# Other memory slots for the gate, staging and product buffers of a planned kernel, and finer cells for its DRAM order

## The chip, the core and the metric

The kernel runs on one core of a Trainium2 chip. The metric is the device time of one execution in microseconds, as the median of several runs. The core has a matrix engine (PE; its weight loads are listed as PEld), a vector engine (DVE), a scalar engine (ACT), a general engine (POOL) and SyncE (SP), whose queue issues nearly all DMA transfers here. Every engine takes its instructions strictly in order, so an instruction that waits holds back everything behind it on that engine.

## The reference

What is computed is attention, then a gated feed-forward layer, then a second feed-forward layer:

```python
# attention, (B, H, S, D) = (4, 8, 576, 64)
scores = where(causal, -1e9, q @ k.T / sqrt(D) + minimum(-(cum[:, None] - cum[None, :]), 0))   # cum = cumsum(max(s, 0))
x = (softmax(scores) @ v) reshaped to (2304, 512)
# layer 1: 512 -> 1536 -> 512
xn = x / sqrt(mean(x * x) + 1e-6) * rms_g
y = (silu(xn @ w_gate) * (xn @ w_val)) @ w_out
# layer 2: 512 -> 2048 -> 512
h = y @ w_in
out = (h / (1 + exp(-1.702 * h))) @ w_out2
```

The weights come as 64-bit floats and are turned into 32-bit floats on the core. Products are made from a high and a low part of each factor, three matmuls for one product.

## The kernel before

The work has two phases. In the first, the 32 heads of attention run, and beside them the first four of the twelve chunks of layer 1 (`G0 = 4`) for tokens 0 to 1727, in seven tiles (`fa_tile`, line 695; tile 6 is the last, 192 tokens wide). Each tile takes tanh on ACT, and writes its result from the buffer `YO` to the DRAM buffer `y_d`, two halves for each tile.

The second phase starts with a job called P: chunk 4 of layer 1 for tokens 0 to 767, straight (8 products, each of 6 matmuls of 384 columns). `gate` takes Silu of a product into one of the two gate buffers `SG0` and `SG1`; `gated` multiplies it with the other product and splits the result into high and low part. Then two matmuls only keep PE going (`ones`), and eight outputs (`Down("P", ...)`, 3 matmuls each) are added to `MK0` and `MK1`, which hold what `y_d` has for these tokens (loaded by two transfers). After P comes R (`run_r`): chunks 0 to 3 for the 576 tokens that the first phase left, in two halves of 288 tokens (`RN`), R0 and R1. At the end of each half four results of 288 tokens, q = 0 to 3, are copied by ACT from PSUM to a staging buffer and written to DRAM (`r_d`). The staging buffers of R0 are `RE`, `M51`, `V1`, `M50` in turn, those of R1 are `RE`, `M51`, `RE`, `M51` (line 1070). Between R1's outputs the first group of the steady part is begun, and that part runs to the end: groups of seven products (`m1` to `m7`, a Strassen form), in which `V1` and the two `M5` buffers carry copies of products. `m3` adds onto the PSUM bank that `m5` has filled, so it can't start before ACT's copy of that bank into `M5` has been made; the next group's `m1` follows `m3`.

Buffers share memory in slots (`SLOTS`, line 32). A slot has turns: its second list of names takes the memory when the first list is no longer used by anyone, which includes DMA transfers that read it. Before, `SG0 SG1` follow `TH0 TH1 YO` in slot `se`; `V1 RE` follow `BT0 BT1` in slot `sa` (`BT` takes half of a head's result from PSUM). Here the names of the profile are those of the slots: `se`, `sa`, `sh` (M5), `sc` (MK), `sb` (the first results of `gated`), `s` for those with a number.

The order of all instructions is made by the program itself, before it emits them. `op` collects what an operation reads and writes as cells (`cells`, 512 bytes in DRAM before, 64 in the on-chip memory), and makes it wait for earlier writers and readers of the same cells and for the users of the turn before in its slot. `plan` then orders the operations on each engine by modelled costs and by the latest time at which each may start. Table loads of ACT have no cost in it; a DMA transfer is modelled as 2.2 us and its bytes at 360 GB/s, one after the other. What the instructions really wait for is worked out separately from the emitted order and the bytes that they touch. The matmuls of the second phase (`tmul`) keep the order in which they are written.

A row of `r_d` is 288 floats, 1152 bytes, and a row of `y_d` 1728 floats, 6912 bytes; neither is a multiple of 512, both are of 128. With cells of 512 bytes the end of a row and the start of the next share a cell.

Of the kernel before, what the change touches and what calls it, by code (L numbers as in the profile page):

```python
# [29 lines left out]
    "VIRT": 260096,  # L30
    "SLOTS": {
# [5 lines left out]
    },  # L37
    "BANK": {"s": (0, 1, 5), "t": (2, 3), "v": (4,), "g": (6,), "o": (7,), "r": (4, 4)}, "BANKX": {"s": (7,), "v": (6,)}, "NX": 8,
    "FB": (0, 1, 2, 3, 4, 5), "BB": (6, 7),
# [8 lines left out]
def attention_then_swiglu_then_gelu(ctx: ExitStack, tc, qT, kT, vp, s, w1, w2, gT, out):  # L48
# [4 lines left out]
    KT = DM // P  # L53
# [9 lines left out]
    H2 = 384  # L63
    NP = NT // (2 * H2)
    RN = (NT - TA) // 2
    NAMES = ["B11", "T1", "T2", "B22", "T3", "B21", "T4"]
# [32 lines left out]
    def few(n):  # L99
# [8 lines left out]
    SHAPE = {  # L108
        "Q": [S], "K": [S], "mask": [S], "SQ": [S], "VS": [5, 2 * D], "PA": [1600], "PT": [512], "VT": [5, 2, D],
        "BT": [320], "XH": [2, TS], "TH": [TS], "FH": [2, TS], "YO": [2, TS], "w": [2, 512], "wb": [512], "ws": [512],  # L110
        "MK": [2, 2, H2], "HH": [2, H2], "M5": [H2], "SG": [H2], "V1": [H2], "RE": [H2], **{nm: [2, 2, H2] for nm in NAMES},
    }
    ROUND = ("QA", "QB", "KA", "KB", "VT", "XH", "FH", "w", "HH", *NAMES)

# [47 lines left out]
    def get(name, n=None):  # L162
        if n is None:
            return BUF[name][0]
        return [BUF[f"{name}{i}"][0] for i in range(n)]

    QS, KS, QB, KB, QA, KA, VS, VT, BT, TH = (get(x, 2) for x in ("QS", "KS", "QB", "KB", "QA", "KA", "VS", "VT", "BT", "TH"))
    mask, SQ, SQT, YO = (get(x) for x in ("mask", "SQ", "SQT", "YO"))
# [3 lines left out]
    WS = [own(f"w{i}", [2, 512], F32R) for i in range(PRM["NWO"])] + [BUF[f"w{i}"][0] for i in range(PRM["NWO"], NWS)]  # L172
    PC = {nm: BUF[nm][0] for nm in NAMES}
    MK, HH, M5, SG = get("MK", 2), get("HH", 8), get("M5", 2), get("SG", 2)
    wb, ws, V1, RE = (get(x) for x in ("wb", "ws", "V1", "RE"))
    FB = [PB[i] for i in PRM["FB"]]
    BB = [PB[i] for i in PRM["BB"]]

# [37 lines left out]
    def size(ap):  # L216
        return 8 if ap.dtype == I64 else 4

    def cells(ap):
        if not hasattr(ap, "offset"):  # L220
            ap = ap[tuple(slice(None) for _ in ap.shape)]
        t, pat, es = ap.tensor.name, tuple(ap.ap), size(ap)
        key = (t, ap.offset, pat, es)
        if key in known:
            return known[key]
        space = str(ap.space)
        if "DRAM" in space and t != virtual.tensor.name:
            offs = [ap.offset * es]
            dims = pat[1:] if pat[0][1] == P else pat
            for st, n in dims[:-1]:  # L230
                offs = [o + st * es * i for o in offs for i in range(n)]
            st, n = dims[-1]
            got = {(t, c) for o in offs for c in range(o // 512, (o + st * es * (n - 1)) // 512 + 1)}
        else:
            pitch, rows = pat[0]
            p0, col = divmod(ap.offset, pitch)
            if "PSUM" in space:
                got = {(t, 0)}
            else:
                offs = [col * es]  # L240
                for st, n in pat[1:-1]:
                    offs = [o + st * es * i for o in offs for i in range(n)]
                st, n = pat[-1]
                half = ([0] if p0 < 64 else []) + ([1] if p0 + rows > 64 else [])
                got = set()
                g = 4 if t == small.tensor.name else 64
                for o in offs:
                    for c in range(o // g, (o + max(st * es * (n - 1), 0) + es - 1) // g + 1):
                        for h in half:
                            got.add((t, c, h))  # L250
                if any(t == x.tensor.name for x in ST):
                    par = [offs[0] // 4 % 2] if st == 2 and es == 4 else [0, 1]
                    got = {x + (y,) for x in got for y in par}
        known[key] = got
        return got
# [51 lines left out]
    def op(eng, fn, cost=None, r=None, w=None, due=None, chain=False, dma=False):  # L307
# [10 lines left out]
        if w is None:  # L318
            for name, kw in rec.calls:
                for k, x in kw.items():  # L320
                    if isap(x):
                        (wr if k in OUTS else rd).update(cells(x))
                if dma:
                    n = size(kw["out"])
                    for x in kw["out"].shape:
                        n *= x
                    o["byts"] += n
        else:
            for x in w:
                wr.update(cells(x))  # L330
            for x in r or ():
                rd.update(cells(x))
# [38 lines left out]
    def cp(o_, i_, scale=1.0, **kw):  # L371
        op("A", lambda e: e.activation(out=o_, in_=i_, func=AF.Copy, scale=scale), **kw)
# [10 lines left out]
    def dma(o_, i_, eng="S", **kw):  # L383
        op(eng, lambda e: e.dma_start(out=o_, in_=i_), dma=True, **kw)
# [533 lines left out]
    def done(b):  # L918
        bank_free.append(b)
# [32 lines left out]
    def add(o_, x, y, o=ALU.add):  # L952
        tt(o_, x, y, o, eng="V")
# [79 lines left out]
    class Down:  # L1033
# [30 lines left out]
        def finish(self, first, final):  # L1064
            self.part(self.chunks)
            b, p, o = self.b, self.p, self.o
            ps = FB[b]
            if self.layer == "R":
                q = o[1]
                t = (RE, M5[1], V1, M5[0])[q % (4 if p == 0 else 2)]  # L1070
                cp(t[:, :RN], ps[:, :RN])
                dma(r_d[p][:, q, :], t[:, :RN])
            elif self.layer == "P":
                t, q = o
                mt = MK[t].rearrange("p a k n -> p (a k) n").bitcast(F32)
                add(mt[:, q, :], ps[:, :H2], mt[:, q, :])
                if q == KT - 1:
                    dma(y_d[:, :, (2 * p + t) * H2:(2 * p + t + 1) * H2], mt)
            elif self.layer == "1":
                t, q = o  # L1080
                y = xT[:, q, (2 * p + t) * H2:(2 * p + t + 1) * H2]
                add(y, ps[:, :H2], y)
            else:
                b0 = p * 2 * H2
                if o < 4:
                    v, src = xT[:, o, b0:b0 + 512], ps[:, :]
                else:
                    k = o - 4
                    v = xT[:, 2 * k:2 * k + 2, b0 + 512:b0 + 768]
                    src = ps.rearrange("p (s f) -> p s f", s=2)  # L1090
                if first:
                    cp(v, src)
                else:
                    add(v, src, v)
                if final:
                    q = p * 6 + o
                    dst = out[q * P:q * P + P, :]
                    dma(dst if o < 4 else dst.rearrange("p (s f) -> p s f", s=2), v)
            done(b)
# [12 lines left out]
    n = 0  # L1112
# [20 lines left out]
    for nm in ("B11", "B21", "B12", "B22"):  # L1133
        k, t = BL[nm]
# [80 lines left out]
    for j, job in enumerate(SJ):  # L1215
        layer, p, cs = job
# [52 lines left out]
    def lat(x, y):  # L1269
        return 0.22 if x != y else 0.0 if x == "T" else 0.06  # L1270

    def length(o):
        return 2.2 + o["byts"] / 360e3 if o["byts"] else min(o["cost"])
# [10 lines left out]
    def plan(asap):  # L1284
# [11 lines left out]
        byasap = {e: sorted((o["i"] for o in ops if e in o["eng"]), key=lambda i: asap[i]) for e in engs}  # L1296
        ptr = {e: 0 for e in engs}
        start, finish, chosen = [None] * N, [None] * N, [None] * N
        count = 0
        stall = []  # L1300
# [10 lines left out]
        while count < N:  # L1311
# [55 lines left out]
            for s_ in o["succ"]:  # L1367
                left[s_] -= 1
                rdy[s_] = max(rdy[s_], finish[i] + lat(e, ops[s_]["eng"]))
                if not left[s_]:  # L1370
                    for k in ops[s_]["eng"]:
                        ready[k].append(s_)
        return start, finish, chosen, stall

    asap = [0.0] * N
    for o in ops:
        t = max([asap[d] + length(ops[d]) + lat(ops[d]["eng"], o["eng"]) for d in o["deps"]], default=0.0)
        asap[o["i"]] = max(t, ideal.get(o["i"], 0.0))
    start, finish, chosen, stall = plan(asap)
    for _ in range(PRM["PASS"]):  # L1380
        start, finish, chosen, stall = plan(start)
# [65 lines left out]
```

## Time and profile before

| | |
|---|---|
| median of 3 runs | 1074.27 us (1073.88 to 1076.59) |
| the profiled execution | 1073.97 us, its span 1072.2 us |
| granted PE clock over the span | 0.987 |
| busy PE, PEld | 1033.4 us (96%), 967.8 us (90%) |
| busy DVE, ACT, POOL | 717.6 us (67%), 577.9 us (54%), 436.9 us (41%) |
| PE not busy | 38.8 us |
| DMA | 165.59 MB, mean 154 GB/s |

The span runs from the first to the last instruction; 1.8 us of the execution lie outside it. The first phase ends at about 350 us, P and R run from there to about 425 us, the rest is the steady part. Nearly all instructions are emitted through one helper, line 206, so a row is told by the tiles that it writes and reads.

### The profile page before, as it was taken

To read this page: it belongs to the slowest core of one execution; us is meant where nothing else is said; L and a number is where in the kernel's file an instruction comes from. 1 tells how busy PE (TensorE), PEld (TensorE's weight loads), DVE (VectorE), ACT (ScalarE), POOL (GpSimd) and SP (SyncE) were. 2 spreads that over 40 slices of the span, in tenths; PEclk is the share of its full clock that TensorE was granted. 3 is DMA by queue.
4 is the path that set the end of the run, shared out by engine and by line. 5 is a ranking of instruction groups with operands and counts; after the bars stand their busy time and mean duration, and the time that the engine had idled before them with its cause. 6 is when DMAs were issued, how large, how long until landed. Compare 5 with 4: busy or idle time off the path is not lost.

```text
span 1072.2 us, 17418 instructions
## 1 busy us (share of the span) xinstructions
PE 1033.4 (96%) x6200; PEld 967.8 (90%) x6200; DVE 717.6 (67%) x1589; ACT 577.9 (54%) x1335; POOL 436.9 (41%) x503
## 2 busy tenths in 40 slices
PE   6998889999999899799999999999999999999998
PEld 4887879999999889799999999999998889999987
DVE  5766878888877756678764678888565377364333
ACT  4776777777776435455433344577563255343222
POOL 5567588878765332535410244543131033030000
PEclk9998999999999989899999999999999999999999
DMA  4334443334311544568275158675255427613551
GB/s 143 101 92 124 143 128 102 88 114 116 98 32 40 171 157 149 202 212 316 62 265 206 40 174 330 246 291 207 98 168 202 160 67 278 225 40 121 206 204 59
DMA packets 59227, 165.59 MB, mean 154 GB/s; under 512 B 6482, under 2 KB 25426, under 8 KB 59140
## 3 DMA queue, kind: packets, MB, share of 16 engines
q1 hardware_dynamic: 59028, 164.40, 44.6%
q8 instruction: 49, 0.80, 0.3%
q14 instruction: 38, 0.31, 0.1%
q10 hardware_dynamic: 112, 0.08, 0.0%
HBM read 117.24 MB, written 44.26 MB: 151 GB/s over the span
## 4 chain that ended last, share of the span: by engine, by line
PE 89%; DVE 4%; DMA 3%; POOL 2%; issue 1%; ACT 1%; SPq 0%; POOLq 0%; ACTq 0%; DVEq 0%
PE b L206 89%; DMA st<-in_w_dram 2%; DVE s L206 1%; POOL s L206 1%; DVE xT L206 1%; DMA s<-s 1%; DMA y_d<-se 0%; DVE se L206 0%; DVE wm L206 0%; DVE sg L206 0%; DVE w L206 0%; DMA s<-c_d 0%; POOL sg L206 0%; ACT w L206 0%; POOL w L206 0%
## 5 line engine op out<-in xcount | busy, mean ns | idle before, releaser
L206 PE MATMUL b<-s,w 128*128 128x384 f32 (+1 forms) x882 | 170.1, 335 | 5.4 <-ACT sh L206 5.4
L206 PEld LDWEIGHTS b<-s,w 128*128 128x128 f32 x882 | 155.0, 190 | 6.4 <-ACT sh L206 5.8
L206 POOL TENSOR_TENSOR wa<-wa,st 128x512 int32<-128x512 int32 x52 | 71.9, 1383 | 205.3 <-ACT sb L206 61.0
L206 DVE TENSOR_TENSOR xT<-b,xT 128x384 f32<-128x384 f32 (+1 forms) x134 | 80.2, 608 | 83.2 <-PE b L206 81.9
L206 PE MATMUL b<-sc,w 128*128 128x256 f32 (+3 forms) x840 | 131.3, 297 | 3.1 <-ACT w L206 2.0
L206 PEld LDWEIGHTS b<-sc,w 128*128 128x128 f32 x840 | 116.1, 193 | 5.1 <-ACT w L206 2.2
L206 PE MATMUL b<-sd,w 128*128 128x256 f32 (+3 forms) x642 | 111.3, 305 | 0.4 <-DVE sd L206 0.3
L206 ACT ACTIVATE b<-b 128x384 f32<-128x384 f32 x119 | 55.6, 479 | 98.5 <-DVE b L206 58.5
L206 POOL TENSOR_SCALAR wm<-wm 128x512 f32<-128x512 f32 x68 | 46.9, 689 | 131.7 <-DVE wm L206 130.4
L206 PE MATMUL b<-s 128*128 128x288 f32 (+4 forms) x384 | 88.2, 357 | 12.7 <-DMA s<-s 9.2
L206 POOL TENSOR_SCALAR s<-s,small 128x576 f32<-128x576 f32 (+4 forms) x160 | 86.3, 558 | 27.3 <-DVE small L206 25.2
L206 PEld LDWEIGHTS b<-sd,w 128*128 128x128 f32 x642 | 96.0, 189 | 1.4 <-DVE sd L206 1.0
L206 ACT ACTIVATE s<-s,small 128x320 f32<-128x320 f32 (+4 forms) x160 | 88.3, 553 | 12.2 <-DVE small L206 11.7
L206 PE MATMUL b<-s,s 128*128 128x384 f32 (+1 forms) x453 | 91.2, 338 | 0.0
L206 PEld LDWEIGHTS b<-s,s 128*128 128x128 f32 x453 | 79.5, 188 | 1.2
L206 PEld LDWEIGHTS b<-s 128*128 128x128 f32 x384 | 60.1, 198 | 22.3 <-issue 9.4
L206 DVE CUSTOM_DVE_ANT_0 s<-b,s 128x448 f32<-128x448 f32 (+4 forms) x160 | 64.5, 425 | 19.5 <-PE b L206 18.1
L206 ACT ACTIVATE se<-b 128x384 f32<-128x384 f32 (+4 forms) x92 | 41.7, 455 | 65.6 <-PE b L206 37.5
L206 ACT ACTIVATE sa<-b 128x384 f32<-128x384 f32 (+2 forms) x93 | 41.8, 451 | 60.3 <-PE b L206 56.6
L206 PE MATMUL b<-w,sc 128*128 128x512 f32 x270 | 74.2, 390 | 0.0
L206 PE MATMUL b<-ident,s 128*128 128x128 f32 x480 | 70.3, 274 | 0.3 <-POOL s L206 0.2
L206 ACT ACTIVATE st<-st 128x512 int32<-128x512 uint32 x68 | 45.8, 675 | 41.8 <-DMA st<-in_w_dram 41.6
(152 smaller groups left out, 2264.8 us busy)
## 6 DMA issues: line engine op xcount, KB each, us to landing
st<-in_w_dram SPq DMA_DIRECT2D x68, 512.0 KB
s<-in_qT_dram SPq DMA_DIRECT2D x52, 144.0 KB
s<-in_kT_dram SPq DMA_DIRECT2D x52, 144.0 KB
s<-pc21B SPq DMA_DIRECT2D x9, 768.0 KB
s<-pc11B SPq DMA_DIRECT2D x6, 768.0 KB
s<-pc22B SPq DMA_DIRECT2D x6, 768.0 KB
out_dram<-xT SPq DMA_DIRECT2D x18, 256.0 KB
s<-in_vp_dram SPq DMA_DIRECT2D x16, 256.0 KB
```

The lines of the kernel that those rows point to most:

```text
L206: return lambda *args, **kw: f(*[real(x) for x in args], **{k: real(x) for k, x in kw.items()})
```

## The change

Three things are changed. The gate buffers move to slot `sa` (after `BT0 BT1`), and `V1` goes to slot `se` (after `TH0 TH1 YO`). The staging buffer of the 288-token results becomes three buffers of that size: `RE0` beside `V1` in `se`, `RE1` and `RE2` beside `ws` in `s5` (after `SQ SQT`); they are used in turn over both halves, and `V1` and `M5` are no longer used for staging. The cells by which the planner tells whether two DRAM accesses touch each other have 128 bytes in place of 512. The widths of the slots stay as they are.

```diff
     "SLOTS": {
-        "s4": ["mask", "wb"], "s5": ["SQ SQT", "ws"], "s6": ["PA0", "T1"], "s7": ["PA1", "B22"], "s8": ["PA2", "B21"],
-        "s9": ["VS0 VS1", "w16"], "sa": ["BT0 BT1", "V1 RE"], "sb": ["VT0 VT1", "HH0 HH1"],
+        "s4": ["mask", "wb"], "s5": ["SQ SQT", "ws RE1 RE2"], "s6": ["PA0", "T1"], "s7": ["PA1", "B22"], "s8": ["PA2", "B21"],
+        "s9": ["VS0 VS1", "w16"], "sa": ["BT0 BT1", "SG0 SG1"], "sb": ["VT0 VT1", "HH0 HH1"],
...
-        "se": ["TH0 TH1 YO", "SG0 SG1"], "sf": ["PT0 PT1 PT2", "T4"], "sg": ["PT3 PT4 PT5", "T2"], "sh": ["PT6 PT7", "M50 M51"],
+        "se": ["TH0 TH1 YO", "V1 RE0"], "sf": ["PT0 PT1 PT2", "T4"], "sg": ["PT3 PT4 PT5", "T2"], "sh": ["PT6 PT7", "M50 M51"],
...
-        "MK": [2, 2, H2], "HH": [2, H2], "M5": [H2], "SG": [H2], "V1": [H2], "RE": [H2], **{nm: [2, 2, H2] for nm in NAMES},
+        "MK": [2, 2, H2], "HH": [2, H2], "M5": [H2], "SG": [H2], "V1": [H2], "RE": [RN], **{nm: [2, 2, H2] for nm in NAMES},
...
-    wb, ws, V1, RE = (get(x) for x in ("wb", "ws", "V1", "RE"))
+    wb, ws, V1 = (get(x) for x in ("wb", "ws", "V1"))
+    RE = get("RE", 3)
...
-            got = {(t, c) for o in offs for c in range(o // 512, (o + st * es * (n - 1)) // 512 + 1)}
+            got = {(t, c) for o in offs for c in range(o // 128, (o + st * es * (n - 1)) // 128 + 1)}
...
-                t = (RE, M5[1], V1, M5[0])[q % (4 if p == 0 else 2)]
+                t = RE[(q + p * KT) % 3]
```

## Rows read from the trace of the kernel before

**Rows 1.** The page, part 1: busy time and share of the span of each engine
```profile
PE 1033.4 (96%) x6200; PEld 967.8 (90%) x6200; DVE 717.6 (67%) x1589; ACT 577.9 (54%) x1335; POOL 436.9 (41%) x503
```

**Rows 2.** What PE waited for: us in total, times, longest
```profile
PE b L206 <- ACT sb L206: 5.6, 1, 5.6
PE b L206 <- ACT sh L206: 5.4, 1, 5.4
PE b L206 <- DVE xT L206: 5.3, 5, 2.8
```

**Rows 3.** The chain that ended last: start us, us, what
```profile
368.81 5.06 DMA y_d<-se
...
373.94 1.21 ACT L206
...
426.67 9.69 DMA st<-in_w_dram
...
463.62 604.85 PE b L206 x3203
```

**Rows 4.** Timeline about the first idle: start, us, engine, [idle before <- releaser]
```profile
351.54 0.42 DVE L206 TENSOR_TENSOR xT<-b,sa 64x256 f32<-64x256 f32 x1
...
360.05 0.33 ACT L206 ACTIVATE se<-b 128x192 f32<-128x192 f32 x1 [2.37 <-PE b L206]
...
360.05 0.60 SPq L206 DMA_DIRECT2D sc<-y_d  x1
...
370.49 0.64 SPq L206 DMA_DIRECT2D sc<-y_d  x1
...
368.55 2.35 PE L206 MATMUL b<-s,s 128*128 128x384 f32 x12
...
373.63 0.75 DVE L206 TENSOR_TENSOR sd<-xT,sd 128x576 fp32r<-128x576 f32 x1
...
377.65 0.69 PE L206 MATMUL b<-sb,s 128*128 128x384 f32 x1 [5.64 <-ACT sb L206]
...
384.04 0.95 PE L206 MATMUL b<-sg,w 128*128 128x288 f32 x6
```

**Rows 5.** Stretches: us, busy us (x) of five engines, granted clock, DMA share
```profile
376.00:378.00 2.00, 0.35 (x1) 0.29 (x1) 2.00 (x4) 1.98 (x5) 2.00 (x2) 0.50 0.59 245
...
380.00:382.00 2.00, 2.00 (x9) 2.00 (x9) 1.19 (x3) 0.00 (x0) 1.50 (x1) 0.60 0.00 0
...
442.00:444.00 2.00, 2.00 (x10) 2.00 (x10) 1.08 (x2) 1.49 (x3) 0.44 (x1) 0.74 0.64 236
```

**Rows 6.** Timeline about the second idle, columns as in rows 4
```profile
430.33 1.20 PE L206 MATMUL b<-sg,w 128*128 128x384 f32 x6
431.37 1.21 PE L206 MATMUL b<-sf,s 128*128 128x384 f32 x6
438.01 4.21 PE L206 MATMUL b<-s,w 128*128 128x384 f32 x12 [5.43 <-ACT sh L206]
...
435.22 0.41 ACT L206 ACTIVATE sh<-b 128x288 f32<-128x288 f32 x1 [2.72 <-DMA r<-sh]
...
436.96 0.61 ACT L206 ACTIVATE w<-wa 128x512 fp32r<-128x512 f32 x1
...
437.61 0.69 DVE L206 TENSOR_TENSOR w<-wa,w 128x512 fp32r<-128x512 f32 x1 [0.67 <-ACT w L206]
...
434.70 1.27 POOL L206 TENSOR_TENSOR wa<-wa,st 128x512 int32<-128x512 int32 x1 [1.74 <-DVE wa L206]
...
420.27 0.32 SPq L206 DMA_DIRECT2D r<-sa  x1
...
422.60 0.58 SPq L206 DMA_DIRECT2D xT<-y_d  x1
...
423.93 0.38 SPq L206 DMA_DIRECT2D r<-sh  x1
```

**Rows 7.** Timeline of POOL ahead of the second idle
```profile
410.45 0.72 POOL L206 TENSOR_SCALAR wm<-wm 128x512 f32<-128x512 f32 x1 [22.84 <-DVE wm L206]
```

## The prediction

> **What bounds the kernel now.** I read the page's busy shares first: PE is busy for 1033.4 us of a span of 1072.2 us [rows 1]. So the time is PE's work, and 38.8 us in which it stands still. Second, the list of what PE waited for: besides the start-up and many small waits there are two single long ones, 5.6 us for ACT writing `sb` and 5.4 us for ACT writing `sh` [rows 2]. Third, the chain that ended last: from 463.62 us on it is PE alone, 604.85 us [rows 3]. No wait of another engine behind that point costs anything, and whatever brings PE to it earlier is kept in full, as long as no transfer or conversion falls behind. Then the timeline about the two waits, with the granted clock.
>
> The first idle lies between P's products and P's outputs. P's last products end at 368.55 + 2.35 = 370.90, some small matmuls follow, and PE stops for 5.64 us until 377.65 [rows 4]. The chain gives the reason: the last half of tile 6, copied into `YO` (slot `se`) just before, is written to `y_d` from 368.81 on, which takes 5.06 us, and only then may the gate buffers, which take the same slot, be written: ACT's table load for Silu at 373.94, 1.21 us, Silu, the gate, the split [rows 3]. After the stop the granted clock is 0.50, the 1.2 GHz level, and in 380 to 382 still 0.60 on average [rows 5]: with 0.50 and 1.00 as the two levels that is 1.6 us of the 2 at the lower one, so PE works at half speed from 377.65 to 381.6, about 3.95 us, and loses half of that, 2.0 us. R0's first product starts at 384.04 [rows 4].
>
> The second idle lies after R1. PE's work ends at 431.37 + 1.21 = 432.58; `m3` of the second group starts at 438.01 [rows 6]. It waits for ACT's copy into `M5`. On ACT, ahead of that copy, stand R1's last staging copy, which waits until 435.22 for an earlier write out of the same buffer, issued at 423.93 [rows 6], 11.3 us before; and then a weight conversion (`st`) whose load took 9.69 us, from 426.67 to 436.36 [rows 3]. The clock afterwards is 0.74 in 442 to 444 [rows 5], so the lower level lasts until about 443.0: 5.0 us at half speed, 2.5 us lost. This idle costs 5.43 + 2.5 = 7.9 us.
>
> **Gate buffers into `sa`.** The last reader of `BT` there is a DVE addition that ends at 351.54 + 0.42 = 351.96 [rows 4]. That is long before P's first pair of products is complete, and 17 us before that last write is issued. The gate of the first 384 tokens can go beside tile 6, table load included, and its wait is gone. What is late next is the gate of the second 384 tokens. PE needs it after the first four outputs. A matmul of 384 columns costs 1.04/6 = 0.173 us at full clock (start to start of two groups of six, 430.33 and 431.37 [rows 6]). Outputs that start at 377.65 - 5.64 = 372.01 have 12 x 0.173 = 2.1 us of their own, so the second split must be there at 374.1. Its products end at 370.90; Silu, multiply and copy follow. They took from the end of the table load, 375.15 [rows 3], to PE's start at 377.65 in the old order, 2.5 us, which fits (373.4). DVE, though, also scales `xT` and splits `sd` in these microseconds, until 373.63 + 0.75 = 374.38 [rows 4]. Bounds for the new wait: 0 and 3 us (all of that ahead of it); I take 0.8. Without a wait R0 would start at 372.01 + 24 x 0.173 = 376.2 and not at 384.04, 7.85 us earlier; R0 itself needs `sd`, ready at 374.38 and so hidden, by 1.8 us of cover. So this part gives 7.85 - 0.8 = 7.0 us, between 4.8 and 7.9.
>
> One cost is not in the planner's model: if Silu were ordered ahead of tile 6's last tanh, ACT would load tables twice more, 2 x 1.21 us. The last tanh is at 360.05 [rows 4]. No row can show whether the new order puts the gate before it, so the bounds are 0 and 2.4 us; I take 0, since Silu needs two products of P first and tile 6 has the earlier due times. The Trainium skill ("ScalarE: Activation LUTs", section "What ACT_TABLE_LOAD costs") puts a switch at about 2.66 us, half of it a drain beside the load, and advises to finish one set before the next, which speaks against an early gate; by it two more switches would be 5.3 us. The row shows 1.21 us and Silu right behind, so here the drain is not seen.
>
> **Finer cells.** The two loads of `MK` were issued at 360.05 and 370.49 [rows 4]. One of them reads rows of `y_d` whose first bytes share a 512-byte cell with what tile 6 writes, so the planner put it behind both writes of tile 6. With 128 bytes it can go beside the other one at about 360.6. This matters now: outputs at 372 would need it, and a load issued at 370.49 among others that take 5.06 us would land at 375.5 or later, beyond the first addition at about 372.5. With the change I cost it at nothing; if it stayed late, up to 3 us of DVE's queue would be blocked, of which six free PSUM banks hide most. The two `ch_d` writes at the start also stop sharing cells; they were issued back to back already. If the attention part is reordered by this, I bound it by the longest wait of PE there, 2.8 us [rows 2], to either side, and take 0.
>
> **Staging buffers.** R1's last copy no longer waits for the write issued at 423.93: with three buffers in turn it follows the one issued at 420.27, ahead of the load of `xT` from `y_d` at 422.60 [rows 6]. And `M5` is free of staging, so its copy can be made as soon as its product is there, which is the group of matmuls ahead of the one at 430.33 [rows 6]. `m3` then goes at 432.58. What is late next: `m1` of the following group, whose weights were complete only at 437.61 + 0.69 = 438.30 [rows 6]. POOL had finished their raw form at 434.70 + 1.27 = 435.97; behind it come ACT's copy, 0.61, and DVE's 0.69 [rows 6], so 437.4 with the hand-overs is the earliest, if ACT is not first held up by the conversion that waits until 436.36. PE would stop after `m3`, at 432.58 + 1.04 = 433.62, for 3.8 to 4.7 us, and the clock may fall again. Before, `m1` started at about 438.01 + 4.21/2 = 440.1, with 2.9 us of half speed still to come. The gain lies between 0.8 us (weights at 438.3, 5.0 us of half speed behind it: 1.8 us earlier less 1.0 more lost) and 4.2 (437.4, the clock stays: 2.7 us and half of 2.9); I take 1.3, near the first, since the load that holds ACT is not touched. R0 now has three buffers and not four: its fourth copy waits for its first write. Nothing on PE needs that bank for several products; 0, at most 0.5.
>
> **Sum.** 7.0 + 1.3 = 8.3 us from the profiled 1073.97 gives 1065.7; the median stands 0.3 above that execution, so 1066.0 us. Is the gain kept? The weight chain between the idles is paced by PE: POOL stood 22.84 us before it could go on at 410.45 [rows 7], with the weight buffers still being read. It should move along with PE.
>
> **Rivals.**
> (a) Both idles go: the new order also brings the chunk's weights in time, since ACT is no longer held by the staging write. 1073.97 - 7.0 - 7.9 + 0.3 = 1059.4. Against it: POOL's 435.97.
> (b) The first idle is only half removed: the second gate waits the full 3 us, and Silu comes between the tanhs (2.4 us). 1066.0 + 2.2 + 2.4 = 1070.6. For it: DVE is full there (2.00 of 2 us in 376 to 378 [rows 5]).
> (c) It doesn't pay: the weight chain is not paced by PE, so PE arrives 7 us earlier and waits 7 us more at `m1`: 1074. Against it: rows 7.
> (d) Slower: the new order puts a weight conversion ahead of a copy that PE needs, in the two later stretches where `xT` is reloaded from `y_d` (there are three such loads). The load then takes 9.69 us as it did behind the first [rows 3], and PE pays 7.9 us each time: 1066.0 + 15.8 = 1081.8. It decides as soon as two such conversions stand ahead; one alone would just undo the gain (1073.9). Against it: in the old order both later stretches run without a wait [rows 3].
>
> **Chances.** A difference of 0.3%, 3.2 us, is about what a measurement of this kernel can tell from none. Forecast 0.55 (its own range 1062.5 to 1069), (a) 0.17, (b) 0.13, (c) 0.08, (d) 0.07. The range 1058.5 to 1072 leaves out (c), (d) and some tails. Faster by over 0.3%: the first three, less 0.03 of (b): 0.82; within: 0.11; slower: 0.07.
>
> **What would show it.** Step one: no wait of PE for ACT `sb` near 372, clock 1.00 through 372 to 384, Silu before 368, both `sc` loads side by side, R0 starting near 377. Step two: ACT's copy into `sh` right behind its product, a wait of PE for `w` of 3 to 5 us in place of the one for `sh`. Wrong would be a PE wait for DVE beyond 2 us ahead of P's outputs, more than three table loads, or a new wait behind the second idle.

## The result and the profile after

The changed kernel takes 1060.7 us, the median of four runs (1060.67 to 1061.42); the kernel before, beside it, 1075.2 us. The ratio is 0.9867 with a 95% interval of 0.985 to 0.9884. The forecast was 1066.0 us with a range of 1058.5 to 1072.0: the time lies inside, and the way was right, but the gain is 14.5 us where 8.3 were forecast. The span of the profiled execution is 1059.4 us, 12.8 us less than before.

The list of what PE waited for (us in total, times, longest) no longer has the two single waits of [rows 2]. What is left behind the attention part has other names:

```profile
PE b L207 <- DVE xT L207: 6.7, 7, 2.8
...
PE b L207 <- DVE sb L207: 0.5, 1, 0.5
...
PE b L207 <- DVE b L207: 0.3, 1, 0.3
```

Five of the seven waits for `xT`, the 2.8 us among them, lie in the attention part and stand there in the kernel before too; the two new ones are 1.09 us at 374.20 and 0.29 us at 454.24.

The timeline of PE about the first idle answers to [rows 4]:

```profile
352.47 2.93 PE L207 MATMUL b<-sc,w 128*128 128x192 f32 x24 [0.71 <-DVE se L207]
...
372.38 0.73 PE L207 MATMUL b<-w 128*128 128x512 f32 x2
374.20 2.53 PE L207 MATMUL b<-sb,s 128*128 128x384 f32 x13 [1.09 <-DVE xT L207]
377.27 2.20 PE L207 MATMUL b<-sb,s 128*128 128x384 f32 x11 [0.54 <-DVE sb L207]
379.31 0.95 PE L207 MATMUL b<-sg,w 128*128 128x288 f32 x6
```

P's outputs wait 1.09 us and, after four of the eight, 0.54 us, where before they waited 5.64 us at once. ACT and SP show how the order changed:

```profile
360.67 0.33 ACT L207 ACTIVATE se<-b 128x192 f32<-128x192 f32 x1 [1.16 <-PE b L207]
361.01 1.28 ACT L207 ACT_TABLE_LOAD   x1
362.31 0.49 ACT L207 ACTIVATE sa<-b 128x384 f32<-128x384 f32 x1
...
360.60 1.36 SPq L207 DMA_DIRECT2D sc<-y_d  x2
```

The table load stands right behind the last tanh, Silu follows into `sa`, and the two loads of `MK` are issued together. About the second idle [rows 6] PE runs through:

```profile
425.60 1.20 PE L207 MATMUL b<-sg,w 128*128 128x384 f32 x6
426.64 1.20 PE L207 MATMUL b<-sf,s 128*128 128x384 f32 x6
427.68 3.28 PE L207 MATMUL b<-s,w 128*128 128x384 f32 x18
...
425.80 0.49 ACT L207 ACTIVATE sh<-b 128x384 f32<-128x384 f32 x1 [0.55 <-PE b L207]
...
434.81 0.62 ACT L207 ACTIVATE w<-wa 128x512 fp32r<-128x512 f32 x1
```

The copy into `M5` (`sh`) is made at 425.80, right behind its product, and the 18 matmuls of `m3`, `m1` and `m2` follow without a gap. The granted clock is 1.00 in every stretch of 2 us from 372 to 380 and from 426 to 436; before, the lower level had cost 2.0 and 2.5 us [rows 5].

To compare kernels I cut each trace at four marks: the 24 matmuls of tile 6 that DVE `se` releases near 352; R0's first product (288 columns); the third group's `m6` (`b<-sg,w`, 384 columns: 449.78 before, 437.86 after); and PE's last matmul. On each engine the order of instructions is the same in all ten traces up to the first mark, yet that first part took between 349.1 and 354.0 us in the ten traces. The changed kernel alone has 352.47 and 349.85. It is a spread that the change has no part in, and it is larger than some effects below. The parts behind the first mark are steady: two traces of the changed kernel agree to 0.01 us in each.

| kernel | first mark at | to R0 | R0 to third `m6` | from there to the end |
|---|---|---|---|---|
| before | 351.56 | 32.48 | 65.74 | 618.69 |
| after | 352.47 | 26.84 | 58.55 | 617.84 |
| after, once more | 349.85 | 26.84 | 58.56 | 617.85 |
| gate buffers alone | 350.58 | 28.98 | 65.67 | 618.68 |
| staging alone | 351.21 | 32.98 | 58.87 | 617.87 |
| cells alone | 354.04 | 33.49 | 60.24 | 619.01 |
| both slot changes, old cells | 349.10 | 29.90 | 59.08 | 617.80 |
| after, last result in `M5` | 349.78 | 26.84 | 59.88 | 618.97 |
| both slot changes, old cells, two buffers in R1 | 351.80 | 28.95 | 59.57 | 617.84 |
| after, banks turned | 353.95 | 28.17 | 58.57 | 617.86 |

So the 12.8 us of the profiled executions are 5.64 up to R0, 7.19 about the second idle, 0.85 behind it, and 0.91 lost in the first part, which is spread.

### The profile page after: what moved, and what is told of

Read it like the earlier page. It is cut to its first block, busy times and chain, and to the rows that moved or that the text cites. A ratio compares the mean times of both kernels' runs of the same rounds, so it can differ in the third digit from the quotient of the medians.

```text
span 1059.4 us, 17417 instructions
## 1 busy us (share of the span) xinstructions
PE 1031.8 (97%) x6200; PEld 966.2 (91%) x6200; DVE 716.0 (68%) x1588; ACT 577.2 (54%) x1334; POOL 439.9 (42%) x505
## 4 chain that ended last, share of the span: by engine, by line
PE 91%; DVE 5%; DMA 1%; POOL 1%; issue 1%; ACT 0%; POOLq 0%; DVEq 0%
PE b L207 91%; DVE s L207 2%; DVE xT L207 1%; DMA st<-in_w_dram 1%; POOL s L207 1%; DMA s<-s 1%; DVE sd L207 0%; DVE sg L207 0%; DVE se L207 0%; DVE wm L207 0%; DVE b L207 0%; POOL sb L207 0%; DVE sb L207 0%; POOL wa L207 0%; DVE sc L207 0%
## 5 line engine op out<-in xcount | busy, mean ns | idle before, releaser
L207 PE MATMUL b<-s,w 128*128 128x384 f32 (+1 forms) x882 | 167.9, 332 | 0.0
L207 PEld LDWEIGHTS b<-s,w 128*128 128x128 f32 x882 | 152.7, 188 | 0.9 <-DVE s L207 0.3
L207 ACT ACTIVATE se<-b 128x384 f32<-128x384 f32 (+4 forms) x85 | 38.9, 459 | 67.8 <-PE b L207 65.5
L207 ACT ACTIVATE sa<-b 128x384 f32<-128x384 f32 (+2 forms) x98 | 44.0, 448 | 53.1 <-DVE b L207 23.1
```

What stands on the lines that cost most here:

```text
L207: return lambda *args, **kw: f(*[real(x) for x in args], **{k: real(x) for k, x in kw.items()})
```

## The experiments

The theory after the result was: the first idle comes from the slot of the gate buffers; the second comes from the copy into `M5`, which had to wait for a staging write that still read that buffer. Two rivals: that the shared DRAM cells were at work; and that ACT, held by a staging copy, was the cause of the second idle.

**The gate buffers alone.**

```diff
-... "sa": ["BT0 BT1", "V1 RE"], ...
+... "sa": ["BT0 BT1", "SG0 SG1"], ...
...
-... "se": ["TH0 TH1 YO", "SG0 SG1"], ...
+... "se": ["TH0 TH1 YO", "V1 RE"], ...
```

> Only the gate buffers and V1 with the old staging buffer change slots; staging order and 512-byte cells stay as before. Theory: the first idle (5.64 us and 2.0 us of half clock) goes but for a wait of 1 to 2 us, the second idle (5.43 us, with half clock 7.9 us) stays: about 5 to 6 us below before, 1069 to 1070. Rival (cells matter): the second load of the partial results of P still stands behind tile 6's writes and holds DVE, so only about 2 us are gained, 1073.

Measured: 1069.84 us beside 1073.61 for the kernel before (ratio 0.9959, 0.9944 to 0.9975). Up to R0 it takes 28.98 us, 3.5 less than before; the second idle stays. PE in this kernel:

```profile
372.35 3.40 PE L206 MATMUL b<-sb,s 128*128 128x384 f32 x18 [1.08 <-DVE xT L206]
378.40 1.32 PE L206 MATMUL b<-sb,s 128*128 128x384 f32 x6 [2.66 <-DVE sc L206]
...
433.34 5.80 PE L206 MATMUL b<-s,w 128*128 128x384 f32 x18 [5.25 <-ACT sh L206]
```

Six outputs fill the six banks and then PE stops for 2.66 us, until additions to `MK` (`sc`) free one: it goes on at 378.40, as the third of the eight additions has ended at 378.35. DVE is not idle there; the additions stand behind other work in its queue:

```profile
374.01 2.07 DVE L206 TENSOR_SCALAR wm<-wm 128x512 int32<-128x512 int32 x1
376.01 0.94 DVE L206 TENSOR_TENSOR s<-xT,s 128x768 fp32r<-128x768 f32 x1
376.88 3.79 DVE L206 TENSOR_TENSOR sc<-b,sc 128x384 f32<-128x384 f32 x8
```

One of the two `MK` loads is issued at 370.41 here, as before. So the theory holds for the gate buffers, and the rival has a part: without the finer cells some 2 us of the gain are missing.

**Staging alone.**

```diff
-... "s5": ["SQ SQT", "ws"], ...
+... "s5": ["SQ SQT", "ws RE1 RE2"], ...
...
-... "sa": ["BT0 BT1", "V1 RE"], ...
+... "sa": ["BT0 BT1", "V1 RE0"], ...
...
-t = (RE, M5[1], V1, M5[0])[q % (4 if p == 0 else 2)]
+t = RE[(q + p * KT) % 3]
```

> Only the staging changes: three buffers in turn, none of them V1 or M5; gate buffers stay behind TH and YO, cells 512 bytes. Theory: the second idle goes wholly since the copy into M5 no longer stands behind staging: 7 to 8 us below before, 1067 to 1068, and the first idle of 5.6 us is still in the trace. Rival (the second idle went because the first part was planned anew, staging has no share): within 1 us of before, 1074 to 1075.

Measured: 1066.95 us beside 1073.61 (ratio 0.993, 0.9905 to 0.9954). The first idle is still there, 5.58 us; R0 to the third `m6` falls from 65.74 to 58.87 us. The theory holds; that this part was only planned anew because of the first is refuted, since here the first part is as before.

**Finer cells alone.**

```diff
-got = {(t, c) for o in offs for c in range(o // 512, (o + st * es * (n - 1)) // 512 + 1)}
+got = {(t, c) for o in offs for c in range(o // 128, (o + st * es * (n - 1)) // 128 + 1)}
```

> Only the cells are 128 bytes. Theory: both idles have their cause in the slots, so the time stays within 1 us of before (1074 to 1075), with the two loads of P's partial results side by side in the trace. Rival (the shared cells of neighbouring rows held the staging writes back): half or more of the second idle goes, 1068 to 1071.

Measured: 1069.07 us beside 1073.61 (ratio 0.9953, 0.9935 to 0.997). The theory was wrong here, and the rival right: the second idle shrinks from 5.43 to 2.04 us, the clock stays up, and the part falls to 60.24 us, with no slot changed. PE, SP and ACT:

```profile
438.10 3.39 PE L206 MATMUL b<-s,w 128*128 128x384 f32 x18 [2.04 <-ACT sh L206]
...
425.18 0.32 SPq L206 DMA_DIRECT2D r<-sh  x1
...
426.08 0.58 SPq L206 DMA_DIRECT2D xT<-y_d  x1
...
429.30 0.32 SPq L206 DMA_DIRECT2D r<-sh  x1
...
437.56 0.49 ACT L206 ACTIVATE sh<-b 128x384 f32<-128x384 f32 x1 [1.57 <-DMA r<-sh]
```

Before, R1's second write (the first `r<-sh` here) was issued behind the load of `xT` from `y_d` [rows 6]; with finer cells it goes ahead of it. The rows of `r_d` end inside a 512-byte cell, so the planner had taken the four writes of one half for a chain, each waiting for the one before. The first idle stays (6.36 us here).

**Both slot changes, old cells.** The changed kernel with 512 in place of 128 in that line.

> Both slot changes, cells 512 bytes as before. Theory: nearly all of the change: 12 to 14 us below before, 1061 to 1063. Rival (finer cells are needed for P's outputs): a wait of PE of 2 to 4 us ahead of or within P's outputs stays, 1064 to 1066.

Measured: 1061.53 us beside 1073.61 (ratio 0.9887, 0.9864 to 0.991). By the time it is the theory; by the trace the rival's wait is there:

```profile
370.85 3.42 PE L207 MATMUL b<-sb,s 128*128 128x384 f32 x18 [1.08 <-DVE xT L207]
376.91 2.29 PE L207 MATMUL b<-sb,s 128*128 128x384 f32 x6 [2.64 <-DVE sc L207]
```

This profiled execution had the shortest first part of all (349.10), which hides the loss; to R0 it takes 29.90 us, 3.06 more than the changed kernel. So the finer cells are worth 2 to 3 us there once the gate buffers are moved, and 0.5 us (59.08 to 58.55) about the second idle once staging has its own buffers. These figures rest on the parts of the traces: in the whole times the two kernels can't be told apart (ratio 0.9887, 0.9864 to 0.991, against 0.9867, 0.985 to 0.9884).

**The changed kernel once more**, as the base of the next three.

> The changed kernel once more, beside the next three on the same chip: 1060 to 1062, no idle of PE above 1.5 us behind 345 us.

Measured: 1060.56 us beside 1072.62 (ratio 0.9883, 0.9864 to 0.9901), with the same two waits ahead of and within P's outputs, 1.08 and 0.55 us.

**The last result staged in `M5`.**

```diff
-t = RE[(q + p * KT) % 3]
+t = M5[1] if p and q == 3 else RE[(q + p * KT) % 3]
```

> The changed kernel, but R1's last result is staged in M5 as before; that buffer is free then, so the staging copy itself waits for no transfer. Theory (the second idle is the next group's copy into M5 waiting for the staging write that still reads it): PE waits for ACT sh again, 3 to 5 us, 1064 to 1067. Rival (it was ACT held up by a staging copy that waits for an earlier write, and by the late weight load): no such idle, 1060 to 1062.

Measured: 1063.2 us beside 1072.62 (ratio 0.9913, 0.9894 to 0.9932). PE, SP and ACT:

```profile
426.84 3.39 PE L207 MATMUL b<-s,w 128*128 128x384 f32 x18 [1.69 <-ACT sh L207]
...
418.34 0.32 SPq L207 DMA_DIRECT2D r<-sh  x1
...
426.30 0.49 ACT L207 ACTIVATE sh<-b 128x384 f32<-128x384 f32 x1 [1.23 <-DMA r<-sh]
```

The wait for `sh` is back, as the theory has it, and it is the write itself that releases the copy, 8.0 us after its issue. But it is 1.69 us and not 3 to 5: alone, the shared buffer costs 1.33 us in this part and 1.12 behind it.

**Two staging buffers in R1, none of them `M5`, old cells.**

```diff
-t = RE[(q + p * KT) % 3]
+t = RE[1 + q % 2] if p else RE[(q + p * KT) % 3]
```

> Both slot changes with 512-byte cells, but R1 stages in two buffers in turn, not three, none of them M5: its third and fourth copy wait on ACT for the writes two before, as in the kernel before. Theory (the shared M5 is the cause): PE does not wait ahead of the second group's third product; against both slot changes alone at most 1 us is lost, 1061 to 1063. Rival (ACT held up by that wait is the cause): an idle of 4 to 5 us of PE at or right behind that place, 1066 to 1069.

Measured: 1062.96 us beside 1072.62 (ratio 0.9907, 0.9884 to 0.9931). ACT is held by a staging copy that waits for a late write, and PE doesn't stop ahead of `m3`, but 1.31 us later on (0.38 there with three buffers):

```profile
431.35 0.41 ACT L207 ACTIVATE s<-b 128x288 f32<-128x288 f32 x1 [2.14 <-DMA r<-s]
...
436.32 1.32 PE L207 MATMUL b<-sf,w 128*128 128x384 f32 x6 [1.31 <-DVE b L207]
```

The part takes 59.57 us, 0.49 more than with three buffers. So ACT held up, by itself, doesn't make the second idle either.

**The free banks turned.** P's first output takes the bank that the scaling of `xT` reads until 374.15 in the changed kernel; the edit lets it take another.

```diff
     ones()
+    bank_free.append(bank_free.pop(0))
+    bank_free.append(bank_free.pop(0))
     tick()
```

> The changed kernel with the free PSUM banks turned by two places before P's outputs, so that the first of them doesn't take the bank that the scaling of xT still reads. Theory: the wait of 1.09 us for DVE xT goes, but the second split, which PE waited for until 377.27, is then met earlier and takes most of it back: 0 to 1.2 us below the changed kernel. Rival (the bank was all that was late): both waits go, 1.6 us or more below it.

Measured: 1060.27 us beside 1072.62 (ratio 0.9887, 0.9865 to 0.9909). To R0 it takes 28.17 us, 1.33 more than the changed kernel:

```profile
373.74 1.75 PE L207 MATMUL b<-sb,s 128*128 128x384 f32 x9
375.82 0.72 PE L207 MATMUL b<-ident,small 64*128 64x64 f32 x3 [0.33 <-DVE xT L207]
376.46 0.79 PE L207 MATMUL b<-sb,s 128*128 128x384 f32 x3
378.40 3.88 PE L207 MATMUL b<-sb,s 128*128 128x384 f32 x12 [1.15 <-DVE xT L207]
```

The first outputs start at once, the transposes for the scaling are ordered behind them, and the same wait for DVE comes after the fourth output; then the clock falls (0.66 in 378 to 380, 0.50 in 380 to 382). The time, 0.3 us below the changed kernel's, would suit the first expectation, but that is far within the spread of the runs (1059.56 to 1064.07). By the trace neither fits: the wait for DVE has only moved, and nothing is won by turning the banks alone. That the clock fell here and not in the changed kernel is seen, not explained.

## Why the prediction was right, and where it was not

The range held, but the sum did not hold it up. At their upper bounds its two terms give 7.9 + 4.2 = 12.1 us, less than the 12.8 us between the profiled executions and the 14.5 us between the medians. That the time lies inside is owed to a range drawn wide enough for rival (a), not to the sum.

**What bounds.** Right: PE, with two idles and a steady end; what brings PE to the end earlier is kept. The third part fell by 0.85 us besides, as the last wait before the steady end, 0.98 us for POOL writing `sg`, is gone. I hadn't listed it, nor a wait of 0.29 us for `xT` that comes in its place.

**Gate buffers.** Forecast 7.0 us (4.8 to 7.9), measured 5.64 up to R0, together with the cells. The mechanism holds: the gate goes beside tile 6, the clock stays up, no extra table load (three in the trace, as before). The remaining wait, put at 0.8 us, is 1.63, and only its smaller part is what I named. The rest of the shortfall, 0.5 us, is in no wait of PE that the profile shows. The second split was late by 0.54 us; the 1.09 us ahead of it are for a PSUM bank, which the scaling of `xT` and P's first output share, and which I hadn't taken into account. The split was late because DVE spent 1.76 us on a subtraction that took 0.75 before [rows 4]:

```profile
374.06 0.56 DVE L207 TENSOR_TENSOR b<-sa,b 128x384 f32<-128x384 f32 x1
374.53 1.76 DVE L207 TENSOR_TENSOR sd<-xT,sd 128x576 fp32r<-128x576 f32 x1
376.21 0.55 DVE L207 TENSOR_TENSOR sc<-b,sc 128x384 f32<-128x384 f32 x1
376.68 0.54 DVE L207 TENSOR_TENSOR sb<-b,sb 128x384 fp32r<-128x384 f32 x1
...
374.25 1.43 POOL L207 TENSOR_TENSOR sf<-xT,sf 128x576 fp32r<-128x576 f32 x1
```

POOL's subtraction had begun first, and DVE's ended 0.6 us behind it. In the kernel before, DVE's began first, at 373.63, and POOL's was the long one:

```profile
373.72 1.91 POOL L206 TENSOR_TENSOR sf<-xT,sf 128x576 fp32r<-128x576 f32 x1
```

The Trainium skill ("SBUF — State Buffer", section "SBUF: two separate sides") says that a POOL operation that reads SBUF and a DVE operation with two SBUF inputs take a port in turns, each for a whole instruction. Both pairs of rows agree with it, but no run here took POOL's work away to show it.

**Finer cells.** This is the first step that failed. I gave them no term of their own in the sum: I took `MK` for their only matter in the second phase, and six free banks to hide most of a late load. They are worth 2 to 3 us up to R0: without them PE had used up the six banks and stopped for 2.66 and 2.64 us. And alone they take 5.50 us off the part about the second idle, through the staging writes: that rows of `r_d` share cells stands in the kernel's description, and I didn't carry it through to the queue of SP.

**Staging.** The second step that failed, and the larger one: forecast 1.3 us (0.8 to 4.2), measured 7.19 with the rest and 6.87 alone. I held the weights of `m1` to be late next, complete only with DVE's operation at 437.61 [rows 6]. That operation belongs to other weights: in the changed kernel the 18 matmuls from 427.68 on run while ACT's copy of that kind comes at 434.81; so what `m1` reads had been there. From the code, the operation at 437.61 makes the down weight of the same chunk, which nobody needs before its outputs, and what `m1` reads had been written in the kernel before by these:

```profile
422.69 0.62 ACT L206 ACTIVATE w<-wa 128x512 fp32r<-128x512 f32 x1
...
423.35 0.69 DVE L206 TENSOR_TENSOR w<-wa,w 128x512 fp32r<-128x512 f32 x1 [0.77 <-ACT w L206]
```

Without this, the forecast would have been rival (a), 1059.4, which is 1.3 us from the measured time.

**What made the second idle.** Neither of its parts alone: the shared buffer costs 1.7 to 2.0 us of waiting (1.69 and 2.04), ACT held up costs 1.31 elsewhere. In the kernel before they stand in a row: with the writes taken for a chain, the second was issued behind the load of `xT`; its buffer came free 11.3 us later; only then could the last copy be made and the last write issued, at 435.66; and the copy into `M5` came behind that, at 437.48.

```profile
435.66 0.32 SPq L206 DMA_DIRECT2D r<-sh  x1
...
437.48 0.47 ACT L206 ACTIVATE sh<-b 128x384 f32<-128x384 f32 x1
```

Cut at either place, 5.5 or 6.9 of the 7.2 us go. The prediction read this chain rightly up to the weights, but not that the cells had made it.

**Rivals (b), (c) and (d)** didn't come: Silu stands behind the last tanh, what was gained up to R0 was kept behind it, and no later stretch has a new wait over 0.3 us.

## What to carry to other kernels

A planner that orders instructions sees memory only through its model: a granule that does not divide the row makes neighbours wait for each other, and here the cost showed in the order of a queue, far from the code that has the granule. Before naming "what is late next", find by the trace's order which instruction consumes the row; a row of the right kind close to the place may belong to something else. And where the same program spreads by several microseconds in a part that the change doesn't touch, compare parts between marks, not whole times.

## What was not expected of the hardware

A wait of the same length did and did not cost clock: with the gate buffers alone PE waited 2.66 us and its next six matmuls took 1.32 us; with both slot changes it waited 2.64 us and they took 2.29 us, the granted clock at 0.63 and then 0.51. The stretches of 2 us, gate buffers alone first:

```profile
376.00:378.00 2.00, 0.00 (x0) 0.00 (x0) 2.00 (x5) 0.00 (x0) 0.97 (x1) 1.00 0.20 78
...
378.00:380.00 2.00, 1.60 (x10) 1.60 (x11) 2.00 (x5) 0.00 (x0) 1.92 (x2) 1.00 0.84 344
```

Both slot changes, old cells:

```profile
376.00:378.00 2.00, 1.09 (x3) 1.09 (x4) 2.00 (x5) 0.00 (x0) 1.92 (x2) 0.63 0.84 344
378.00:380.00 2.00, 2.00 (x9) 2.00 (x9) 1.57 (x4) 0.00 (x0) 1.25 (x1) 0.51 0.36 134
```

(Columns as in [rows 5]: the granted clock is the third number from the end.) A shorter wait can cost it too: with the banks turned the clock fell behind waits of 0.33 and 1.15 us, while in the changed kernel it stayed at 1.00 behind 1.09 and 0.54 us. What decides it no run here shows.

A small write can be slow. The staging writes of 144 KB gave their buffers back 8.0 us (last result in `M5`), 8.3 us (cells alone, from 429.30 to the copy at 437.56) and 11.3 us (before) after their issue, where they stood behind the load of `xT` and other large transfers. It isn't their size: the write issued at 435.66 in the kernel before must have let go of its buffer by 437.48, when ACT writes that buffer again, so within 1.8 us. That the difference comes from the queue ahead is likely, but no run here isolates it. The Trainium skill ("DMA: Bandwidth & Descriptors", section "Anatomy of one DMA — SWDGE (gpsimd) path") gives about 2.0 us and the bytes at 436 GB/s for one transfer, an estimate of 2.3 us here, for another way of issue; the measured 8.0 to 11.3 us are for transfers issued behind others.
